# The order of the elementwise steps in the second MLP of a convolution and two-MLP kernel, and how far its output products follow

## The chip, the cores and the metric

The kernel runs on one core of a Trainium2 chip. The metric is device time in microseconds (us) of one execution: 1053.47 us before the change, the median of three runs (1053.28 to 1053.54). Within a core TensorE (PE) multiplies, ScalarE (ACT) and VectorE (DVE) do the elementwise work, and SyncE (SP) issues transfers. Each engine works through its own queue in the order in which the program was written; semaphores order the engines against one another.

## The reference

Three stages follow one another over 8192 tokens of 192 features: a causal convolution of 7 taps whose weights are a softmax, an MLP with SiLU, and an MLP with ELU (hidden width 2048 in both).

```python
def _moe_ref(x, w_in, w_out):
    h = x @ w_in
    g = h * (1.0 / (1.0 + np.exp(-h)))
    return (g @ w_out).astype(np.float32)

def _moe2_ref(x, w_in, w_out):
    h = x @ w_in
    alpha = 1.0
    g = np.where(h > 0.0, h, alpha * (np.exp(np.minimum(h, 0.0)) - 1.0))
    return (g @ w_out).astype(np.float32)

def reference(**kwargs):
    ...
    x = attn_out.reshape(B * S, D)
    x = _moe_ref(x=x, **moe_kwargs)
    return _moe2_ref(x=x, **moe2_kwargs)
```

## The kernel before

The tokens are cut into 16 blocks of 512 (`TB`, `NB`), the hidden width into 8 parts of 256 (`NQ`). A unit `u = (layer, b, q)` is one part of one block of one layer: 128 units for the SiLU layer (layer 0), then 128 for the ELU layer (layer 1). To keep precision, inputs, weights and hidden values are scaled by powers of two and held as two 16-bit floats, a high part and a low part (the remainder); products of high with high, high with low and low with high are summed.

A unit has three stages on three engines.

- PE, `in_products`: 18 matmuls that make `h`, 256 hidden rows by 512 tokens, in PSUM. They run as 9 pairs, one on each half of the array's rows. `h` has two buffers, so the products of unit u+2 need u's `h` read.
- ACT and DVE, `act_steps`. In layer 1 these are six steps: ACT copies `h` into `g` ("copy", L639), DVE takes the minimum with zero into `e` ("min", L640), ACT does the exponential of `e` in place ("exp", L643), DVE joins the two, max(e - 1, g), into `g` ("join", L644), ACT writes the scaled 16-bit high part `hi` ("high", L627, tile `g_hi`), and DVE writes the remainder `lo` ("low", L630).
- PE, the out-products: `high_products` (12 matmuls of `hi`, into the sums `c0`, `c1`, `ab0`, `ab1`, L702) and `low_ab` (4 matmuls of `lo`, L724). The rest of the low part, `low_c` (4 matmuls for each unit, L714), is kept for all eight units of a block and done at the block's end.

The order is written by hand in one loop over steps s (`tc.manual_schedule()`). In step s PE gets the in-products of unit s and then the out-products of an earlier unit, `done`: three units back (`LATE`) in most of layer 0 and in layer 1. `act_steps` spreads the six steps of a layer-1 unit over three loop steps. `running` holds what is still to be issued, so that step s puts on the queues first high and low of unit s-2, then exp and join of unit s-1, then copy and min of unit s.

At the step in which `done` is a block's last unit, PE gets `end_products`: 32 `low_c` matmuls, the last `high_products` and `low_ab`. Then the two sums are taken out of PSUM: `end_c` and `end_ab` (an ACT copy with scale and a DVE add each, `both` and `o`), and `emit_end_c` (an ACT copy across rows and a DVE add, `other`). `late = act[3:] * done[0]` puts the second half of the step's list (join, copy, min) behind the sums.

Other work of layer 1 sits at fixed steps before a block's first unit s, by `at(...)`: at s-4 `set_scale` (seven small DVE instructions, ahead of the step's own), at s-3 `split_mid` (two ACT and two DVE instructions that make the block's `x_hl`, behind the step's own, and two SP transfers, L320, that carry half of `x_hl` across the partition halves).

Buffers: in layer 1 `hi` takes half of a tile of `g_hi` or `g_lo` by turns (three tiles each), `g` one of the three `raw` tiles, `lo` one of 11 ring slots, `e` one of two. The four sums have one buffer each.

For the last unit `act_steps` issues all that is left at once, and there the high part is made by DVE (`soon`). Behind the loop stand the out-products of the last three units. In the last block the low part of `ab` is summed only then, by `last_ab` (28 matmuls in two banks).

Of the kernel before, what the change touches and what calls it, by code (L numbers as in the profile page):

```python
# [9 lines left out]
F32 = mybir.dt.float32  # L10
F32R = mybir.dt.float32r
I32 = mybir.dt.int32
I64 = mybir.dt.int64
U16 = mybir.dt.uint16
F16 = mybir.dt.float16
# [9 lines left out]
P = 128  # L25
HP = 64
TB = 512
# [3 lines left out]
NQ = DFF // (2 * P)  # L31
W_IN = 3 * P
W_OUT = 2 * D
# [12 lines left out]
def kernel(  # L46
# [17 lines left out]
    nc = tc.nc  # L64
# [3 lines left out]
    raw = ctx.enter_context(tc.tile_pool(name="raw", bufs=RAW))  # L68
# [6 lines left out]
    gp = ctx.enter_context(tc.tile_pool(name="gp", bufs=3))  # L75
# [364 lines left out]
    def scaled(layer, b):  # L440
        return layer == 1 or b >= NEW
# [82 lines left out]
    def conv_steps(b, g, acc=None):  # L524


        n = HT if g else TB

        def tap(k):
            if k == 0:  # L530
                slot = acc or (lambda: xin.tile([P, TB], F32, tag=f"conv{g}", name="conv")[:, 0:n])
                conv_t[b, g] = slot()
            x, y = x_raw[b][:, g, k : k + n], conv_t[b, g]
            w = tap_w[:, g, k : k + 1]
            if k == 0:
                nc.vector.tensor_scalar_mul(y, x, w)
            else:
                nc.vector.scalar_tensor_tensor(  # L538
                    out=y, in0=x, scalar=w, in1=y, op0=ALU.mult, op1=ALU.add
                )  # L540

        return [lambda k=k: tap(k) for k in range(TAPS)]
# [22 lines left out]
    def weights_of(u, k):  # L565
        layer, b, q = u
        return wt16[q][k] if layer == 0 and b >= NEW else wt[layer, q][k]
# [26 lines left out]
    def products(streams):  # L594
        for pair in zip(*streams):
            for f in pair:
                f()

    running = []

    def act_steps(u):

        h = h_t.pop(u)
        new = scaled(*u[:2])
        hi = gp.tile([P, 2, TB], F32R, tag=f"g_{'lo' if new and where[u] % 2 else 'hi'}", name="g_hi")
        if new:
            hi = hi.bitcast(F16)[:, :, 0:TB]
            lo = ring.tile([P, 2, TB], F16, tag=f"lo{where[u] % RING}", name="lo16")
        else:
            lo = gp.tile([P, 2, TB], F32R, tag="g_lo", name="g_lo")  # L610
        g_t[u] = hi, lo
        if new and u[0] == 1:
            g = raw.tile([P, W_IN + W_OUT], I64, tag="raw", name="g").bitcast(F32)[:, 0 : 2 * TB]
            g = g.rearrange("p (i t) -> p i t", i=2)
        else:
            g = h if u not in in_tmp else tmp.tile([P, 2, TB], F32, tag="g", name="g")
        g_of[u] = g
        if not new:
            return [
                lambda: nc.scalar.activation(out=hi, in_=h, func=ACTF.Silu),  # L620
                lambda: nc.scalar.activation(out=g, in_=h, func=ACTF.Silu),
                lambda: nc.vector.tensor_sub(out=lo, in0=g, in1=hi.bitcast(F32)),
            ]
        s = forth[u[:2]]

        def high():
            nc.scalar.activation(out=hi, in_=g, func=ACTF.Copy, scale=s)  # L627

        def low():
            nc.vector.scalar_tensor_tensor(  # L630
                out=lo, in0=g, scalar=s, in1=hi, op0=ALU.mult, op1=ALU.subtract
            )

        if u[0] == 0:
            silu = lambda: begun.append(nc.scalar.activation(out=g, in_=h, func=ACTF.Silu, scale=h_down[u[:2]]))  # L635
            return [silu, high, low]
        e = tmp.tile([P, 2, TB], F32, tag="g", name="e")
        whole = [
            lambda: begun.append(nc.scalar.activation(out=g, in_=h, func=ACTF.Copy, scale=h_down[u[:2]])),  # L639
            lambda: nc.vector.tensor_scalar_min(e, g, 0.0),  # L640
        ]
        power_of = [
            lambda: nc.scalar.activation(out=e, in_=e, func=ACTF.Exp),  # L643
            lambda: nc.vector.scalar_tensor_tensor(  # L644
                out=g, in0=e, scalar=-1.0, in1=g, op0=ALU.add, op1=ALU.max
            ),
        ]
        if u == (1, 0, 0):
            whole.insert(0, lambda: nc.scalar.activation(out=tap_s, in_=tap_s, func=ACTF.Exp, scale=0.0))
        soon = lambda: nc.vector.tensor_scalar_mul(hi, g, s)  # L650
        before = running.pop(0)[1] if len(running) > 1 else []
        if running:
            before = before + running[0][0]
        if u == units[-1]:
            hi_2, lo_2 = running[0][1]
            return before + whole + [hi_2, power_of[0], lo_2, power_of[1], soon, low]
        running.append((power_of, [high, low]))
        return before + whole

    def open_sums(u):  # L660
        for name in ("c0", "c1", "ab0", "ab1"):
            acc_t[(*u[:2], name)] = ps_a.tile([P, TB], F32, tag=name, name=name)
# [28 lines left out]
    def high_products(u, end_ab=False, end_c=False):  # L691

        layer, b, q = u
        hi, wo = g_t[u][0], weights_of(u, 1)
        if q == 0:
            open_sums(u)
        order = [("c", 1), ("ab", 0), ("ab", 2)]
        order = [(*o, i) for o in order for i in range(2)]

        def product(r, n):  # L700
            name, k, i = order[n]
            nc.tensor.matmul(  # L702
                out=acc_t[layer, b, f"{name}{r}"], lhsT=wo[ROWS[r], i, ts(k, P)], rhs=hi[ROWS[r], i, :],
                start=q == 0 and n in (0, 2), stop=end_ab and n == len(order) - 1 or end_c and n == 1,
            )

        return [[lambda r=r, n=n: product(r, n) for n in range(len(order))] for r in range(2)]

    def low_c(u, last):

        layer, b, q = u
        for i in range(2):
            for r in range(2):
                nc.tensor.matmul(  # L714
                    out=acc_t[layer, b, f"c{r}"][ROWS[i], :], lhsT=weights_of(u, 1)[ROWS[r], i, P:D],
                    rhs=g_t[u][1][ROWS[r], i, :], start=False, stop=last,
                )
# [151 lines left out]
    LAG, LATE = 2, 3  # L869
    SOLE = 7  # L870

    units = [(0, 0, 0), (0, 0, 1), (0, 1, 0), (0, 1, 1)]
# [4 lines left out]
    where = {u: s for s, u in enumerate(units)}  # L877
# [32 lines left out]
    for b in range(2, NB):  # L910
        s = where[0, b, 0]
        if b > 2:
            at(s - 14, lambda b=b: pending.extend(x_loads(b)) if b < 5 else load_x(b))
        steps = [f for fs in zip(*(conv_steps(b, g) for g in range(2))) for f in fs]
# [16 lines left out]
    for b in range(NB):  # L931
        s = where[1, b, 0]
# [26 lines left out]
    for k, q in enumerate(range(NQ)):  # L959
        s = where[0, 8 + k, 0]  # L960
# [5 lines left out]
    with tc.manual_schedule():  # L966
# [174 lines left out]
        for s in range(4, TWO + 3):  # L1141
# [4 lines left out]
            act = act_steps(units[s])  # L1146
# [20 lines left out]
        act = act_steps(units[TWO + 3])  # L1167
# [3 lines left out]
        products(out_products(units[TWO + 1]))  # L1171

        turn = where[0, NEW, 0] + LAG
        for s in range(TWO + 4, n_units):
            u = units[s]
            products(in_products(u))
            act = act_steps(u)
            done = units[s - (LATE if s > turn else LAG)]
            new, late = scaled(*done[:2]), []
            if s == turn or done[2] < NQ - 1:  # L1180
                run_fill(s)
                run(act)
                run_fill(s, 3)
                if s != turn:
                    products(high_products(done) if new else out_products(done))
                    if new and done[:2] != (1, NB - 1):
                        low_ab(done, False)
                continue
            if new:
                run_fill(s, 0)  # L1190
                late = act[3:] * done[0]
                run(act[: len(act) - len(late)])
                end_products(done)
            else:
                run(act[:1])
                products(out_products(done))
            both, end_c, end_ab = end_steps(*done[:2])
            end_c()
            if not new:
                run(act[1:])  # L1200
                run_fill(s, 0, 1)
            end_ab()
            run(late)
            if new:
                run_fill(s, 1)
            emit_end_c(*done[:2], both)
            run_fill(s, 2, 3)

        for u in units[-LATE:-1]:
            products(high_products(u))  # L1210
        for u in units[-NQ:-SOLE]:
            low_ab(u, False)
        for u in units[-NQ:-1]:
            low_c(u, False)
        products(high_products(units[-1], end_ab=True))
        low_c(units[-1], True)
        banks = [(tokens, last_ab(units[-SOLE:], tokens)) for tokens in HALF]
        both, end_c, end_ab = end_steps(1, NB - 1)
        end_ab()
# [47 lines left out]
```

## Time and profile before

| | us |
|---|---|
| median of three runs | 1053.47 |
| the profiled execution | 1051.94 |
| span of its trace, first to last instruction | 1050.1 |
| of that, layer 1 from the end of layer 0's last block on | about 520 |

The profile is one execution. Its page gives busy time by engine and the chain of work that ended last; the trace gives every instruction with its start, its length and what ended the idle time before it. The lengths of matmuls are modelled and overlap, so the pace of TensorE is read from the distance between starts of the same instruction in successive steps or blocks, not from its busy share.

### The profile page before, as it was taken

What the parts mean: (1) busy time and instruction counts of PE and PEld (TensorE: products, weight loads), DVE (VectorE), ACT (ScalarE), POOL (GpSimd) and SP (SyncE); (2) the same over time, 40 slices, a digit from 0 to 9 for tenths busy, and PEclk for the clock granted to TensorE, in tenths of its full rate; (3) what the DMA queues carried; (4) which work ended last, traced back from release to release, by engine and by line L of the source; (5) the groups of instructions that cost most, each with busy time, mean ns of one, the idle gap of its engine ahead of it and who ended that gap; (6) DMA issues with size and microseconds to landing.
All of it is one profiled execution on the core that took longest, in us unless ns stands there. A gap on an engine that the chain in (4) does not pass through costs nothing.

```text
span 1050.1 us, 23168 instructions
## 1 busy us (share of the span) xinstructions
PE 1037.2 (99%) x9763; PEld 543.2 (52%) x9763; DVE 906.9 (86%) x1321; ACT 814.7 (78%) x893; POOL 66.1 (6%) x108
## 2 busy tenths in 40 slices
PE   9999999999999999999999999999999999999996
PEld 6889844444444444444444555545544545555443
DVE  8999789888888888887679889888898888898887
ACT  7765776676777777677778888888888889888885
POOL 5420003102000000000000000000000000000000
PEclk9999999999999999999999999999999999999999
DMA  6411226334433233212122111111011110111000
GB/s 166 137 46 57 51 66 160 93 93 110 103 67 79 39 76 67 52 21 56 47 41 51 27 41 52 50 37 52 16 51 52 37 51 26 42 52 50 17 27 16
DMA packets 46519, 62.31 MB, mean 59 GB/s; under 512 B 10128, under 2 KB 29712, under 8 KB 46416
## 3 DMA queue, kind: packets, MB, share of 16 engines
q1 hardware_dynamic: 42416, 48.00, 18.5%
q0 software_dynamic: 4000, 12.85, 4.8%
q8 instruction: 76, 1.25, 0.5%
q14 instruction: 27, 0.22, 0.1%
HBM read 37.72 MB, written 12.61 MB: 48 GB/s over the span
## 4 chain that ended last, share of the span: by engine, by line
PE 72%; DVE 18%; ACT 6%; issue 3%; DMA 1%; SPq 1%; DVEq 0%
PE h L587 35%; PE ab L702 14%; PE c L702 7%; PE ab L724 7%; DVE lo L630 7%; DVE g L644 6%; ACT g_hi L627 4%; PE c L714 4%; PE ab L777 2%; PE c L777 1%; DVE e L640 1%; PE ab L683 1%; DVE x_hl L352 1%; PE c L683 1%; DVE o L825 1%
## 5 line engine op out<-in xcount | busy, mean ns | idle before, releaser
L587 PE MATMUL h<-x_hl,wi 64*128 64x512 f16 (+1 forms) x2592 | 337.4, 378 | 1.8 <-DMA x_hl<-x_hl 1.4
L587 PE MATMUL h<-x_hl,w 64*128 64x512 f16 x1872 | 220.3, 377 | 1.4 <-ACT w L250 0.7
L630 DVE SCALAR_TENSOR_TENSOR lo<-g,forth,g_hi 128x1024 f16<-128x1024 f32 x128 | 164.2, 1283 | 49.6 <-ACT g_hi L627 49.3
L627 ACT ACTIVATE g_hi<-g,forth 128x1024 f16<-128x1024 f32 x127 | 145.7, 1147 | 68.8 <-DVE g L644 68.8
L587 PEld LDWEIGHTS <-wi 64*128 64x128 f16 x2304 | 134.7, 94 | 122.5 <-issue 9.1
L635 ACT ACTIVATE h<-h,h_down 128x1024 f32<-128x1024 f32 x104 | 113.1, 1087 | 99.1 <-PE h L587 92.0
L630 DVE SCALAR_TENSOR_TENSOR lo<-h,forth,g_hi 128x1024 f16<-128x1024 f32 x104 | 133.4, 1283 | 59.7 <-ACT g_hi L627 59.7
L644 DVE SCALAR_TENSOR_TENSOR g<-e,g 128x1024 f32<-128x1024 f32 x128 | 156.0, 1219 | 1.1 <-ACT e L643 1.1
L587 PEld LDWEIGHTS <-w 64*128 64x128 f16 x1872 | 94.0, 94 | 110.1 <-issue 1.5
L702 PE MATMUL ab<-g_hi,wo 64*128 64x512 f16 x1024 | 142.9, 376 | 0.0
L639 ACT ACTIVATE g<-h,h_down 128x1024 f32<-128x1024 f32 x128 | 140.3, 1096 | 1.3 <-PE h L587 1.3
L702 PEld LDWEIGHTS <-wo 64*128 64x128 f16 x1536 | 85.0, 94 | 95.6 <-issue 21.7
L643 ACT ACTIVATE e<-e 128x1024 f32<-128x1024 f32 x128 | 133.2, 1041 | 0.8 <-DVE e L640 0.8
L627 ACT ACTIVATE g_hi<-h,forth 128x1024 f16<-128x1024 f32 x104 | 115.8, 1113 | 3.4
L702 PE MATMUL ab<-g_hi,w 64*128 64x512 f16 x832 | 107.0, 377 | 0.0
L538 DVE SCALAR_TENSOR_TENSOR conv<-x_raw,tap_w,conv 128x512 f32<-128x512 f32 (+1 forms) x174 | 102.9, 631 | 0.2
L702 PEld LDWEIGHTS <-w 64*128 64x128 f16 x1248 | 60.7, 94 | 75.2 <-issue 5.3
L640 DVE TENSOR_SCALAR e<-g 128x1024 f32<-128x1024 f32 x128 | 88.0, 688 | 2.1 <-ACT g L639 2.1
L702 PE MATMUL c<-g_hi,wo 64*128 64x512 f16 x512 | 84.9, 377 | 4.5 <-ACT g_hi L627 4.1
L724 PE MATMUL ab<-lo,wo 64*128 64x512 f16 x484 | 82.4, 377 | 0.0
L702 PE MATMUL c<-g_hi,w 64*128 64x512 f16 x416 | 62.3, 377 | 0.0
L724 PE MATMUL ab<-lo,w 64*128 64x512 f16 x416 | 62.1, 377 | 0.0
(146 smaller groups left out, 1061.4 us busy)
## 6 DMA issues: line engine op xcount, KB each, us to landing
raw<-in_w_dram POOLq DMA_DIRECT2D x16, 512.0 KB, 7.0
x_hl<-x_hl SPq DMA_DIRECT2D x62, 128.0 KB, 2.4
x_raw<-in_xT_dram SPq DMA_DIRECT2D x16, 259.0 KB, 6.1
kept_ab<-mid_ab SPq DMA_DIRECT2D x16, 256.0 KB, 2.0
raw<-in_w_dram POOLq DMA_DIRECT2D x32, 128.0 KB, 5.9
mid_ab<-kept_ab SPq DMA_DIRECT2D x16, 256.0 KB, 3.1
mid_c<-kept_c SPq DMA_DIRECT2D x32, 128.0 KB, 3.1
out_dram<-o SPq DMA_DIRECT2D x15, 256.0 KB, 2.0
```

The lines of the kernel that those rows point to most:

```text
L538: nc.vector.scalar_tensor_tensor(out=y, in0=x, scalar=w, in1=y, op0=ALU.mult, op1=ALU.add)
L587: nc.tensor.matmul(out=h[:, r, :], lhsT=w[ROWS[r], w_lo, ts(of, P)], rhs=x_part(layer, b, 3 * x_lo + part)[ROWS[r], :], start=n == 0, stop ...
L627: nc.scalar.activation(out=hi, in_=g, func=ACTF.Copy, scale=s)
L630: nc.vector.scalar_tensor_tensor(out=lo, in0=g, scalar=s, in1=hi, op0=ALU.mult, op1=ALU.subtract)
L635: silu = lambda: begun.append(nc.scalar.activation(out=g, in_=h, func=ACTF.Silu, scale=h_down[u[:2]]))
L639: lambda: begun.append(nc.scalar.activation(out=g, in_=h, func=ACTF.Copy, scale=h_down[u[:2]])),
L640: lambda: nc.vector.tensor_scalar_min(e, g, 0.0),
L643: lambda: nc.scalar.activation(out=e, in_=e, func=ACTF.Exp),
L644: lambda: nc.vector.scalar_tensor_tensor(out=g, in0=e, scalar=-1.0, in1=g, op0=ALU.add, op1=ALU.max),
L702: nc.tensor.matmul(out=acc_t[layer, b, f"{name}{r}"], lhsT=wo[ROWS[r], i, ts(k, P)], rhs=hi[ROWS[r], i, :], start=q == 0 and n in (0, 2), ...
L714: nc.tensor.matmul(out=acc_t[layer, b, f"c{r}"][ROWS[i], :], lhsT=weights_of(u, 1)[ROWS[r], i, P:D], rhs=g_t[u][1][ROWS[r], i, :], start=F ...
L724: nc.tensor.matmul(out=acc_t[layer, b, f"ab{r}"], lhsT=weights_of(u, 1)[ROWS[r], i, 0:P], rhs=g_t[u][1][ROWS[r], i, :], start=False, stop= ...
```

## The change

In layer 1 a step now issues copy and min of unit s first, then exp and join of unit s-1, then high and low of unit s-2. At a block's end the sums go on the queues ahead of that step's high and low (`late = act[-2:] * u[0]`), not ahead of join, copy and min. Out-products run four units behind instead of three from the fourth unit of layer 1 on; for that one step (`next_turn`) issues no out-products.

Two neighbouring units share one `g_hi` tile for their high parts, each in one half of it, and odd units take a `g_lo` tile for `g`, so that `hi` and `g` have six places each (`hi` had six, `g` three).

The last unit's high part is made by ACT, and the last steps are ordered by hand anew. Behind the loop stand the out-products of four units.

```diff
@@ act_steps
+        side = where[u] % 2
+        if u[0] == 0 or not side:
+            hi = gp.tile([P, 2, TB], F32R, tag=f"g_{'lo' if new and side else 'hi'}", name="g_hi")
+            hi_pair[:] = [hi.bitcast(F16)]
         if new:
-            hi = hi.bitcast(F16)[:, :, 0:TB]
+            hi = hi_pair[0][:, :, ts(side * u[0], TB)]
...
         if new and u[0] == 1:
-            g = raw.tile([P, W_IN + W_OUT], I64, tag="raw", name="g").bitcast(F32)[:, 0 : 2 * TB]
-            g = g.rearrange("p (i t) -> p i t", i=2)
+            if side:
+                g = gp.tile([P, 2, TB], F32R, tag="g_lo", name="g").bitcast(F32)
+            else:
+                g = raw.tile([P, W_IN + W_OUT], I64, tag="raw", name="g").bitcast(F32)[:, 0 : 2 * TB]
+                g = g.rearrange("p (i t) -> p i t", i=2)
...
-        soon = lambda: nc.vector.tensor_scalar_mul(hi, g, s)
-        before = running.pop(0)[1] if len(running) > 1 else []
-        if running:
-            before = before + running[0][0]
+        steps = whole + (running[-1][0] if running else [])
+        if len(running) > 1:
+            steps += running[-2][1]
+        running.append((power_of, [high, low]))
         if u == units[-1]:
-            hi_2, lo_2 = running[0][1]
-            return before + whole + [hi_2, power_of[0], lo_2, power_of[1], soon, low]
-        running.append((power_of, [high, low]))
-        return before + whole
+            (hi_1, lo_1), (hi_2, lo_2), steps = running[-2][1], steps[-2:], steps[:-2]
+            steps += [*power_of, hi_2, hi_1, lo_2, high, lo_1, low]
+        return steps
@@ the loop
+        next_turn = where[1, 0, 0] + LATE
...
-            done = units[s - (LATE if s > turn else LAG)]
+            done = units[s - LAG - (s > turn) * (LATE - LAG) - (s > next_turn)]
...
-                if s != turn:
+                if s not in (turn, next_turn):
                     products(high_products(done) if new else out_products(done))
...
-                late = act[3:] * done[0]
+                late = act[-2:] * u[0]
@@ behind the loop
-        for u in units[-LATE:-1]:
-            products(high_products(u))
+        products(high_products(units[-4]))
         for u in units[-NQ:-SOLE]:
             low_ab(u, False)
-        for u in units[-NQ:-1]:
+        for u in units[-NQ:-3]:
             low_c(u, False)
+        for u in units[-3:-1]:
+            products(high_products(u))
         products(high_products(units[-1], end_ab=True))
-        low_c(units[-1], True)
+        for u in units[-3:]:
+            low_c(u, u == units[-1])
```

## Rows read from the trace of the kernel before

**Rows 1.** The page: busy time by engine, and the chain's shares by engine.
```profile
PE 1037.2 (99%) x9763; PEld 543.2 (52%) x9763; DVE 906.9 (86%) x1321; ACT 814.7 (78%) x893; POOL 66.1 (6%) x108
PE 72%; DVE 18%; ACT 6%; issue 3%; DMA 1%; SPq 1%; DVEq 0%
```
**Rows 2.** Stretches of a block, layers 0 and 1: length, busy by engine, clock, DMA.
```profile
499.64:530.95 31.31, 31.31 (x307) 14.03 (x305) 19.14 (x29) 23.10 (x24) 0.00 (x0) 1.00 0.19 44
850.92:882.92 32.00, 31.97 (x307) 16.24 (x306) 28.54 (x37) 27.66 (x30) 0.00 (x0) 1.00 0.15 42
```
**Rows 3.** The chain in order of time, one unit of layer 1: start, us, what.
```profile
848.15 1.15 DVE g L644
...
849.33 1.16 ACT g_hi L627
...
850.51 1.28 DVE lo L630
851.79 1.15 DVE g L644
```
**Rows 4.** Timeline of TensorE, starts of blocks' `low_c`: start, us, [idle before].
```profile
530.95 1.92 PE L714 MATMUL c<-lo,w 64*64 64x512 f16 x32
...
562.39 1.92 PE L714 MATMUL c<-lo,wo 64*64 64x512 f16 x32
...
1010.88 1.92 PE L714 MATMUL c<-lo,wo 64*64 64x512 f16 x32
```
**Rows 5.** Timeline of TensorE, in-products: a block's end step, and an ordinary step.
```profile
528.91 2.11 PE L587 MATMUL h<-x_hl,wi 64*128 64x512 f16 x18
...
534.54 2.11 PE L587 MATMUL h<-x_hl,wi 64*128 64x512 f16 x18
...
538.21 2.11 PE L587 MATMUL h<-x_hl,wi 64*128 64x512 f16 x18
...
541.88 2.10 PE L587 MATMUL h<-x_hl,wi 64*128 64x512 f16 x18
```
**Rows 6.** Timeline of ScalarE, one step of layer 1 and a sum.
```profile
850.38 1.04 ACT L643 ACTIVATE e<-e 128x1024 f32<-128x1024 f32 x1
851.33 1.09 ACT L639 ACTIVATE g<-h,h_down 128x1024 f32<-128x1024 f32 x1
...
854.97 0.67 ACT L834 ACTIVATE both<-c,back 128x512 f32<-128x512 f32 x1
```
**Rows 7.** Timeline of VectorE: `min`, first of `set_scale`, the step behind it, a split.
```profile
861.76 0.69 DVE L640 TENSOR_SCALAR e<-g 128x1024 f32<-128x1024 f32 x1
862.36 0.41 DVE L484 TENSOR_REDUCE total<-all 128x1 f32<-128x256 f32 x1
...
863.71 1.28 DVE L630 SCALAR_TENSOR_TENSOR lo<-g,forth,g_hi 128x1024 f16<-128x1024 f32 x1
...
870.28 0.75 DVE L352 SCALAR_TENSOR_TENSOR x_hl<-mid_ab,x_up,x_hl 128x512 f16<-128x512 f32 x1
```
**Rows 8.** Crossing of `x_hl`: ACT's second write, SP's issue, TensorE, landing times.
```profile
773.22 0.71 ACT L351 ACTIVATE x_hl<-mid_c,x_up 128x512 f16<-128x512 f32 x1
...
774.54 1.30 SPq L320 DMA_DIRECT2D x_hl<-x_hl  x2
...
776.96 1.24 PE L587 MATMUL h<-x_hl,wi 64*128 64x512 f16 x9
779.33 1.24 PE L587 MATMUL h<-x_hl,wi 64*128 64x512 f16 x9 [1.13 <-DMA x_hl<-x_hl]
...
DMA to landing us min/median/max: 2.0/2.4/5.1
```
**Rows 9.** Timeline of TensorE, the end of the kernel.
```profile
1037.60 0.61 PE L702 MATMUL c<-g_hi,wo 64*128 64x512 f16 x4 [2.16 <-ACT g_hi L627]
...
1039.43 1.71 PE L714 MATMUL c<-lo,wo 64*64 64x512 f16 x28
...
1042.81 3.23 PE L741 MATMUL last<-lo,wo 128*128 128x256 f16 x28
```

More of the change, by code (lines that the diff above doesn't have):

```diff
@@ L599 @@
     running = []
+    hi_pair = []
     def act_steps(u):
@@ L604, in act_steps @@
         new = scaled(*u[:2])
-        hi = gp.tile([P, 2, TB], F32R, tag=f"g_{'lo' if new and where[u] % 2 else 'hi'}", name="g_hi")
+        side = where[u] % 2
+        if u[0] == 0 or not side:
+            hi = gp.tile([P, 2, TB], F32R, tag=f"g_{'lo' if new and side else 'hi'}", name="g_hi")
+            hi_pair[:] = [hi.bitcast(F16)]
         if new:
-            hi = hi.bitcast(F16)[:, :, 0:TB]
+            hi = hi_pair[0][:, :, ts(side * u[0], TB)]
             lo = ring.tile([P, 2, TB], F16, tag=f"lo{where[u] % RING}", name="lo16")
```

## The prediction, made before the change was run

> **What bounds the kernel now.** I read the page first. It shows TensorE at 99% and a chain of which 72% is TensorE [rows 1], which would leave an elementwise reordering nothing to win. But matmul lengths are modelled and overlap, so I looked at the pace next. The same eight units take 31.31 us in layer 0 and 32.00 us in layer 1, both "full" by TensorE's busy time, at a granted clock of 1.00, the full 2.4 GHz, both times [rows 2]. Both blocks have the same matmuls in number and size. So 0.69 us of each layer-1 block is not TensorE's own work. TensorE's own pace in layer 1 is seen just behind the layer boundary, before the other engines have fallen back: an ordinary step takes 541.88 - 538.21 = 3.67 us and a block's end step 534.54 - 528.91 = 5.63 us [rows 5]; 7 x 3.67 + 5.63 = 31.32 us, which is layer 0's block.
>
> What takes the 32.00 us is in the chain: late in layer 1 it holds no TensorE at all, only join (DVE), high (ACT), low (DVE), join again, 3.64 us a turn [rows 3]. That is a ring closed by the order of the queues. Low of unit s-2 waits for high of the same unit, join of s-1 stands behind that low on DVE, and the next high waits for that join. ACT and DVE are busy for only 27.66 and 28.54 us of the block [rows 2], but neither can use its free time, because each waits for the other. The ring's 3.64 us is just under TensorE's 3.67 us, so it loses nothing in an ordinary step. What stands on the ring besides (the sums, `set_scale`, the split) it cannot win back, and so the ring, not TensorE, sets 32.00 us a block.
>
> **The ordinary step.** Nothing is added or removed: three ACT and three DVE instructions per unit, as before. In the new order a step's first instruction, copy, waits for TensorE; min waits for this copy; exp needs the min of the step before, high the join of the step before, and low the high just ahead. Nothing that ACT waits for in a step is made by DVE in the same step, so the ring is open. ACT then needs 1.09 + 1.04 + 1.16 = 3.29 us [rows 3, 6], DVE 0.69 + 1.15 + 1.28 = 3.12 us [rows 3, 7], both under TensorE's 3.67. The price is that copy, behind which exp and high are queued, now waits for TensorE at the head of ACT's queue. That costs nothing as long as the out-products come late enough: high of unit u is written in step u+2 and read in step u+4, more than one step of 3.67 us later. With three units behind, that reserve would be a fraction of a step; the fourth unit is its cover.
>
> **The end step.** From the start of its in-products: they end at 1.94, copy at 3.0, exp at 4.1. TensorE finishes `c` at 1.94 + 1.86 (the `low_c`) + 0.43 = 4.2 and `ab` at 5.5. ACT's two sums take 0.67 each [rows 6], DVE's I take at 0.75, as the split of the same size [rows 7]: `c` is free at 5.7, `ab` at 7.0. The next block writes them at 5.5 + 1.94 = 7.5 and at 7.9. So 0.9 us are left for `ab`, the tightest place on PSUM. High, behind the sums now, ends at 7.4, low at 8.7; they are needed at 11.1 and 12.4.
>
> **Scale and split.** `set_scale` takes 863.71 - 862.36 = 1.35 us of DVE [rows 7] a step after the sums, the split 1.5 us a step later. With them DVE needs 4.5 and 4.6 us in two steps of 3.67, and runs up to 2 us behind; it wins 0.55 us a step back over the rest of the block. By the same walk low is then still some 2.6 us ahead of TensorE's need for it. DVE's backlog also moves the crossing of `x_hl`. Adding the lengths up (other ends at 9.4, `set_scale` at 10.8, two steps' work at 17.0, the split at 17.8), SP issues it 2.4 us ahead of the next block's first in-products, at 20.2. With the instructions overlapping at their ends, as they do in the timeline, it is 3.1. Before, it is 776.96 - 774.54 = 2.42 us [rows 8]. TensorE needs it 0.97 us into these in-products. The second transfer goes out 0.65 us behind the first and lands 2.4 us later in the median, 5.1 at worst [rows 8]. So the median has room, and a stray one like the 1.13 us wait in rows 8 stays possible. I count nothing for it, and 0 to 2 us in the range.
>
> **The buffers.** Six places for `g` instead of three, and as many for `hi`: the reader of a place is done steps before the next writer. That two units share a tile, in interleaved halves, could order a write of one half behind a read of the other. Before, ACT writes the third part of `x_hl` at 773.22 while the transfer that reads parts one and four of the same tile goes out only at 774.54, and does not wait for it [rows 8]: interleaved parts are kept apart. I take 0; the other end is in the rivals.
>
> **The sum.** (1) Blocks. From the `low_c` of layer 1's first block to that of its 15th are 1010.88 - 562.39 = 448.49 us [rows 4]. At 31.31 us, 14 blocks take 438.34: **-10.15**. (2) The fourth unit. The first `low_c` comes one unit later in the stream, and the step ahead of it has in-products only: 534.54 + 1.94 + 7 x 3.67 + 2.04 = 564.21 against 562.39 [rows 4, 5]: **+1.82**. (3) The end. From the last `low_c` in the loop to the last matmul are now 1042.81 + 3.23 - 1010.88 = 35.16 us [rows 4, 9], with waits such as the 2.16 us for high, because the ring paces the last steps too, whose TensorE work is short. A pair of matmuls is 3.67 / 17 = 0.216 us. New: the rest of the end step 3.59; four steps of 15 pairs (the last block leaves out `low_ab`), 12.96; then high 1.30, `low_ab` 0.43, five units' `low_c` 1.22 (20/28 of 1.71), three times high 3.89, three units' `low_c` 0.73, `last_ab` 3.23 [rows 9]. Together 27.35: **-7.81**. I walked the elementwise steps beside this. The last copy ends 1.1 us after the last in-products; the three highs that are left end 4.1, 5.1 and 6.2 us after them and are needed at 4.2, 5.6 and 6.8; the last low ends at about 8.0 and is needed at 8.1. DVE's high, 0.75 us shorter to wait for in principle, is not missed. This fits so closely that 0.5 us may be lost. What follows the last matmul, 1050.1 - 1046.04 = 4.06 us, stays.
>
> Sum: -16.1 us. The profiled execution goes from 1051.94 to 1035.8 us. The median of the runs is 1.53 us above the profiled one; I keep that and forecast **1037.3 us**, 1.5% less.
>
> **A rule weighed.** 17 pairs in 3.67 us are 216 ns for each pair of 512 columns, at the granted clock of 1.00, step after step [rows 2, 5], also in layer 0, where ACT is busy for only 23 of 31 us. The Trainium skill (TensorE: Matmul & The Clock Gate, Back-to-back issue gap) gives a formula that comes to the same 216 ns, but calls it the gap of isolated matmuls and says that a sustained stream reaches about 131 ns; by that TensorE would have no floor at 3.67 us and the sum would end at DVE's busy time. The trace speaks against it: no step shorter than the formula's is seen in either layer. It stands as the last rival.
>
> **Rivals and chances.**
> (a) Forecast, TensorE bound at 31.2 to 31.5 us a block, 1034.5 to 1041 us: 0.84. TensorE's pace beside elementwise engines that no longer pause is not in the trace; the nearest rows bound it by 31.31 (layer 0) and, if half of what layer 1 loses stays, 31.65 [rows 2].
> (b) Part of the loss stays at one place per block, the `ab` bank with its 0.9 us or the crossing: 0.4 us x 14 = 5.6, giving 1043. Against it: both walks leave room. 0.06.
> (c) The shared tile orders halves after all. Then the first products behind the loop, due 1.3 us after the last in-products, wait for the neighbour's high, ready at 4.1: 2.8 us, giving 1040. 0.03.
> (d) Another ring takes the place of the old and nothing changes, 1053.5: it would need DVE to make within a step what ACT waits for in it, and no pair of steps does. 0.03.
> (e) Slower: the crossing. If DVE's backlog leaves 3.75 us from issue to need, and both transfers land as late as the worst row, 0.65 + 5.1 = 5.75, TensorE stands 2.0 us in each of 15 blocks: +30, 1067 us. It outweighs the gain from 1.1 us a block on, a landing of 4.2 us every time. The median is 2.4, and one of 15 blocks shows a wait. 0.03.
> (f) TensorE is faster once fed: DVE's 28.5 us a block would bind, 14 x 2.8 = 39 us less again, 998 us. 0.01.
>
> Faster by over 0.2% (about what a measurement of this kernel tells from no change) hold (a), (b), (c) and (f): 0.94. Within: 0.03. Slower: 0.03. For 8 in 10 the range takes in (a)'s bounds and reaches over (b) and (c): 1034 to 1043.5 us.
>
> **What the profile after would show.** Blocks of layer 1 at 31.3 us between `low_c` starts; a chain of TensorE down to the last products, without DVE-ACT rings; ACT idle ahead of copy, released by TensorE; DVE idle by some 2.8 us a block, mostly ahead of min and low; no waits of 2 us for high at the end, and about 27.4 us from the last `low_c` of the loop to the last matmul. Blocks still at 32.0 with idle TensorE ahead of the first in-products would mean (b) or (e); waits on `g_hi` ahead of even units' out-products (c).

## The result and the profile after

The changed kernel takes 1038.2 us in the median (four runs, 1037.97 to 1038.64) against 1053.49 us before: a ratio of 0.9856, 95% interval 0.9839 to 0.9873, 1.4% less. The forecast was 1037.3 us. The profiled execution took 1037.99 us; its span is 1036.3 us, 13.8 us under the span before.

The page of the changed kernel, busy time by engine and the chain's shares, beside [rows 1]:

```profile
PE 1028.6 (99%) x9763; PEld 524.5 (51%) x9763; DVE 908.1 (88%) x1320; ACT 818.5 (79%) x894; POOL 66.1 (6%) x108
PE 95%; DVE 2%; ACT 1%; issue 1%; DMA 0%; SPq 0%; POOL 0%; DVEq 0%; POOLq 0%
```

TensorE's busy share is 99% in both kernels and says nothing. The chain says it: TensorE's part went from 72% to 95%, DVE's from 18% to 2%. The same in one block of layer 1 (stretch: length, busy time of PE, PEld, DVE, ACT, POOL, granted clock, DMA), beside [rows 2]:

```profile
816.84:848.15 31.31, 31.31 (x306) 14.03 (x304) 28.72 (x37) 27.88 (x29) 0.00 (x0) 1.00 0.15 43
```

The elementwise engines do the same 28.7 and 27.9 us of work, in 31.31 us instead of 32.00. That is layer 0's block. What ACT waits for in the 14 blocks from the first `low_c` of layer 1 to the last, first in the kernel before, then in the changed one (the list of waits: us in total, times, longest):

```profile
ACT g_hi L627 <- DVE g L644: 60.1, 98, 1.2
```

```profile
ACT g L646 <- PE h L587: 33.3, 57, 0.9
ACT o L840 <- PE ab L730: 8.5, 14, 0.6
ACT both L840 <- PE c L708: 4.5, 14, 0.3
```

Before, high waited for DVE's join, 98 times; now ACT waits for TensorE alone. The ring is gone and the order of waiting is the one wanted: elementwise work behind TensorE. The chain in order of time shows it in the changed kernel's ordinary step, beside [rows 3]:

```profile
827.93 1.94 PE h L587 x18
829.88 0.43 PE c L708 x4
830.31 0.86 PE ab L708 x8
831.17 0.43 PE ab L730 x4
831.60 1.94 PE h L587 x18
```

831.60 - 827.93 = 3.67 us, TensorE with no pause. Starts of `low_c` in the timeline of TensorE, beside [rows 4]; the first is that of layer 0's last block, the last that of layer 1's 15th:

```profile
530.88 1.92 PE L720 MATMUL c<-lo,w 64*64 64x512 f16 x32
...
565.98 1.92 PE L720 MATMUL c<-lo,wo 64*64 64x512 f16 x32
...
597.29 1.92 PE L720 MATMUL c<-lo,wo 64*64 64x512 f16 x32
...
628.98 1.92 PE L720 MATMUL c<-lo,wo 64*64 64x512 f16 x32
...
848.15 1.92 PE L720 MATMUL c<-lo,wo 64*64 64x512 f16 x32
...
879.74 1.92 PE L720 MATMUL c<-lo,wo 64*64 64x512 f16 x32
...
1004.98 1.92 PE L720 MATMUL c<-lo,wo 64*64 64x512 f16 x32
...
1029.31 3.23 PE L747 MATMUL last<-lo,wo 128*128 128x256 f16 x28
```

Twelve of the 14 blocks take 31.31 us; the two that end at 628.98 and 879.74 take 31.69 and 31.59. From these rows the 13.8 us divide as follows.

| | before | after | difference | forecast |
|---|---|---|---|---|
| first `low_c` of layer 1 at | 562.39 | 565.98 | +3.59 | +1.82 |
| from there to the 15th `low_c` | 448.49 | 439.00 | -9.49 | -10.15 |
| from there to the end of the last matmul | 35.16 | 27.56 | -7.60 | -7.81 |
| from there to the end of the span | 4.06 | 3.76 | -0.30 | 0 |
| sum | | | -13.80 | -16.14 |

The 2.3 us that are missing lie in the first two lines. All but about 0.1 us of them are waits for the crossing of `x_hl`; the worst is at layer 1's second block. The transfer's issue on SP, and TensorE's in-products of that block, beside [rows 8]:

```profile
550.69 1.30 SPq L320 DMA_DIRECT2D x_hl<-x_hl  x2
...
551.17 1.04 PE L587 MATMUL h<-x_hl,wi 64*128 64x512 f16 x8
553.18 0.37 PE L587 MATMUL h<-x_hl,wi 64*128 64x512 f16 x1 [0.97 <-DMA x_hl<-x_hl]
553.81 1.24 PE L587 MATMUL h<-x_hl,wi 64*128 64x512 f16 x9 [0.25 <-DMA x_hl<-x_hl]
```

Here the crossing goes out only 0.48 us ahead of the in-products. The next in-products start at 556.41, 5.24 us behind these instead of 3.67. In the next block the lead is 584.25 - 581.33 = 2.92 us:

```profile
581.33 1.30 SPq L320 DMA_DIRECT2D x_hl<-x_hl  x2
...
584.25 2.10 PE L587 MATMUL h<-x_hl,wi 64*128 64x512 f16 x18
```

One reason stands in DVE's timeline ahead of it: between low and the next min, DVE finds the maximum of layer 0's last block (two reductions, 541.50 to 542.69) and then does `set_scale`, 2.5 us in one piece, and everything behind it comes later, the split too.

```profile
541.50 0.68 DVE L423 TENSOR_REDUCE sum<-mid_ab 128x1 f32<-128x512 f32 x1
542.09 0.67 DVE L423 TENSOR_REDUCE sum<-other 64x1 f32<-64x512 f32 x1
542.69 0.40 DVE L484 TENSOR_REDUCE total<-all 128x1 f32<-128x256 f32 x1
...
544.01 0.69 DVE L647 TENSOR_SCALAR e<-g 128x1024 f32<-128x1024 f32 x1
```

In the two blocks that take 31.69 and 31.59 us the lead is 2.92 us too, but there the two transfers land 3.6 and 3.5 us after their issue (the median of the pair), where 2.4 is usual.

### The profile page after: what moved, and what is told of

Same layout as the page of the kernel before. It is cut to its first block, busy times and chain, and to the rows that moved or that the text cites. A ratio compares the mean times of both kernels' runs of the same rounds, so it can differ in the third digit from the quotient of the medians.

```text
span 1036.3 us, 23166 instructions
## 1 busy us (share of the span) xinstructions
PE 1028.6 (99%) x9763; PEld 524.5 (51%) x9763; DVE 908.1 (88%) x1320; ACT 818.5 (79%) x894; POOL 66.1 (6%) x108
## 4 chain that ended last, share of the span: by engine, by line
PE 95%; DVE 2%; ACT 1%; issue 1%; DMA 0%; SPq 0%; POOL 0%; DVEq 0%; POOLq 0%
PE h L587 46%; PE ab L708 19%; PE c L708 10%; PE ab L730 9%; PE c L720 5%; PE ab L783 2%; PE c L783 1%; PE ab L689 1%; PE c L689 1%; DMA x_hl<-x_hl 0%; PE warm L977 0%; DVE lo L637 0%; PE conv_ps L1008 0%; DVE g L651 0%; ACT g_hi L634 0%
## 5 line engine op out<-in xcount | busy, mean ns | idle before, releaser
L587 PE MATMUL h<-x_hl,wi 64*128 64x512 f16 (+1 forms) x2592 | 330.0, 378 | 1.4 <-DMA x_hl<-x_hl 1.4
L587 PEld LDWEIGHTS <-wi 64*128 64x128 f16 x2304 | 114.8, 94 | 136.9 <-issue 2.5
L708 PE MATMUL ab<-g_hi,wo 64*128 64x512 f16 x1024 | 133.2, 376 | 0.0
L708 PEld LDWEIGHTS <-wo 64*128 64x128 f16 x1536 | 75.2, 94 | 92.7 <-issue 6.6
L708 PE MATMUL c<-g_hi,wo 64*128 64x512 f16 x512 | 78.1, 377 | 0.0
L730 PE MATMUL ab<-lo,wo 64*128 64x512 f16 x484 | 73.8, 376 | 0.0
```

What stands on the lines that cost most here:

```text
L587: nc.tensor.matmul(out=h[:, r, :], lhsT=w[ROWS[r], w_lo, ts(of, P)], rhs=x_part(layer, b, 3 * x_lo + part)[ROWS[r], :], start=n == 0, stop ...
L708: nc.tensor.matmul(out=acc_t[layer, b, f"{name}{r}"], lhsT=wo[ROWS[r], i, ts(k, P)], rhs=hi[ROWS[r], i, :], start=q == 0 and n in (0, 2), ...
L730: nc.tensor.matmul(out=acc_t[layer, b, f"ab{r}"], lhsT=weights_of(u, 1)[ROWS[r], i, 0:P], rhs=g_t[u][1][ROWS[r], i, :], start=False, stop= ...
```

## Experiments

My theory was that the old order closes a ring of DVE and ACT, that the new order opens it, that four units' distance and six places for `g` are what the new order needs, and that TensorE then sets the pace. The rivals were that the distance alone does it, that the order alone does it, and that the places and the sums are by-work. Each experiment undoes one part of the changed kernel, unless it says otherwise. The kernel before ran beside each group: 1053.62 us (15 runs, 1051.57 to 1054.02) beside the old order, the new order three behind, the three places and the sums; 1052.72 us (7 runs) beside the changed kernel again, the last units in turn, the split and the whole of min more before the change; 1051.9 us (7 runs) beside the other three with more of min.

### The changed kernel again

> The changed kernel once more, beside the next ones on the same chip: 1038.2 us again within 0.5 us, with TensorE waiting for the crossing of layer 1's second block by about 1 us and blocks of 31.31 us otherwise.

Measured: 1038.94 us (four runs, 1037.78 to 1039.36), ratio 0.9871 (0.9854 to 0.9887), 0.2 us more than was expected at most. The profile shows the same two waits for the crossing at layer 1's second block, 0.97 and 0.25 us; of the 14 blocks one is late (31.55 us) instead of two. The runs spread by 1.6 us, which is nearly as much as the effect of the split at the head of its step; that experiment is read from its runs' spread and its trace together.

### The old order, four units behind

```diff
-        steps = whole + (running[-1][0] if running else [])
-        if len(running) > 1:
-            steps += running[-2][1]
+        older = running[-2][1] if len(running) > 1 else []
+        newer = running[-1][0] if running else []
+        steps = older + newer + whole if u != units[-1] else whole + newer + older
...
-                late = act[-2:] * u[0]
+                late = act[3:] * done[0]
```

> The changed kernel with the old order in layer 1's loop (high and low of unit s-2 first, copy and min of unit s last, sums where they were); six places for g, four units behind and the new last unit stay. Theory 1 (the ring join, high, low closed by the order sets the block): blocks of layer 1 go back to 31.9 to 32.5 us, the last steps are paced by the ring again, 1050 to 1057 us in all, with the chain on DVE and ACT. Theory 2 (the gain comes from out-products standing four units behind, which gives TensorE more slack): blocks stay at 31.3, 1037 to 1040 us.

Measured: 1057.7 us (1057.54 to 1058.05), ratio 1.0042 (1.0027 to 1.0057): slower than before the change, with all that the change gives but the order. One block, and the chain inside another:

```profile
859.49:892.19 32.70, 32.00 (x306) 18.82 (x304) 28.64 (x37) 27.78 (x30) 0.00 (x0) 1.00 0.14 42
```

```profile
846.96 1.16 ACT g_hi L634
...
848.14 1.28 DVE lo L637
849.43 1.15 DVE g L651
...
851.78 1.28 DVE lo L637
```

The ring is back with its 3.64 us a turn (851.78 - 848.14, from low to low) and the block is 32.70 us, 0.2 over what was expected; the time is 0.7 us over its range. Theory 1 holds: the distance alone brings nothing. That it is worse than before the change fits the sums lying one step later, right ahead of `set_scale`, so that the ring carries both in a row; this was read from the chain and not tried by itself.

### The new order, three units behind

```diff
-            done = units[s - LAG - (s > turn) * (LATE - LAG) - (s > next_turn)]
+            done = units[s - LAG - (s > turn) * (LATE - LAG)]
...
-                if s not in (turn, next_turn):
+                if s != turn:
...
-        products(high_products(units[-4]))
```

> The changed kernel with out-products three units behind in layer 1. Theory 1 (the new order needs the fourth unit as cover: high of unit u is written in step u+2 some 3.2 us after the in-products and would be read 3.7 us after them, which DVE's backlog of up to 2 us behind sums, set_scale and split exceeds): blocks of 32.2 to 32.8 us, waits of TensorE for high or low a few times a block, 1050 to 1058 us. Theory 2 (the order alone opens the ring and is enough): 31.3 us a block, 1037 to 1041 us.

Measured: 1052.2 us (1052.12 to 1052.4), ratio 0.9993 (0.9983 to 1.0003): no gain at all. Blocks take 32.18 us (822.34, 854.51, 886.70). TensorE's waits, and one of them in its timeline:

```profile
PE ab L730 <- DVE lo L637: 7.5, 15, 1.6
```

```profile
869.54 0.61 PE L730 MATMUL ab<-lo,wo 64*128 64x512 f16 x4 [0.43 <-DVE lo L637]
```

Fifteen waits in 15 blocks, each for a low. In the block shown the listed wait is 0.43 us of the 0.87 that the block is over 31.31; the rest is in small pauses of the same step and the two before it, which take 3.72, 3.88 and 4.27 us. The chain leads from that low back along DVE, `set_scale` in it, to the sums of the block just ended: DVE's backlog, as the prediction had it. Theory 1 holds: order and distance only work together.

### Three places for g

```diff
-            if side:
-                g = gp.tile([P, 2, TB], F32R, tag="g_lo", name="g").bitcast(F32)
-            else:
-                g = raw.tile([P, W_IN + W_OUT], I64, tag="raw", name="g").bitcast(F32)[:, 0 : 2 * TB]
-                g = g.rearrange("p (i t) -> p i t", i=2)
+            g = raw.tile([P, W_IN + W_OUT], I64, tag="raw", name="g").bitcast(F32)[:, 0 : 2 * TB]
+            g = g.rearrange("p (i t) -> p i t", i=2)
```

> The changed kernel with g in the three raw tiles only, as before the change. Theory 1 (the new order then closes another ring: copy of unit u+3, first in ACT's step, must wait for low of unit u, last in DVE's step before, so copy, exp, high, low stand in line, about 4.4 us a step): 36 to 38 us a block, 1110 to 1140 us, ACT's copy waiting for DVE's low. Theory 2 (the places are only a convenience, three are enough because a unit lives for three steps): 1038 to 1042 us.

Measured: 1153.37 us (1153.31 to 1153.44), ratio 1.0948 (1.0926 to 1.097). Theory 1 by kind, and more than its range. ACT's largest wait and TensorE's, and the turn of the new ring (timelines of ACT and of DVE):

```profile
ACT g L643 <- DVE lo L634: 164.3, 123, 2.4
PE c L705 <- ACT both L837: 44.3, 15, 3.0
```

```profile
865.08 1.11 ACT L643 ACTIVATE g<-h,h_down 128x1024 f32<-128x1024 f32 x1 [1.51 <-DVE lo L634]
866.10 1.05 ACT L647 ACTIVATE e<-e 128x1024 f32<-128x1024 f32 x1
...
869.69 1.11 ACT L643 ACTIVATE g<-h,h_down 128x1024 f32<-128x1024 f32 x1 [1.51 <-DVE lo L634]
```

```profile
867.17 1.23 DVE L648 SCALAR_TENSOR_TENSOR g<-e,g 128x1024 f32<-128x1024 f32 x1 [0.25 <-ACT e L647]
868.32 1.28 DVE L634 SCALAR_TENSOR_TENSOR lo<-g,forth,g_hi 128x1024 f16<-128x1024 f32 x1
```

Copy waits for the place that low frees, exp follows copy, join waits for exp, low stands behind join, and the next copy waits for it: 869.69 - 865.08 = 4.61 us a turn, 38.4 us a block. I had expected 4.4 by way of high; the ring goes by way of join. ACT, late by that, also takes the sums late, and TensorE waits 3.0 us for them in 15 blocks. So the new order can't do without the six places. Places for `hi` were not taken away by themselves.

### The sums behind high and low

```diff
-                late = act[-2:] * u[0]
+                late = []
```

> The changed kernel with a block's sums behind the step's high and low instead of ahead of them. Theory 1 (ab's bank has 0.9 us to spare, and high and low ahead of the sums take it just about up): 0 to 0.3 us a block, 1038 to 1042 us. Theory 2 (the place of the sums is what frees the block's end): TensorE waits for the banks by about the 1.1 to 1.3 us of a high or low in each block, 1053 to 1057 us.

Measured: 1038.21 us (1037.75 to 1038.62), ratio 0.9856 (0.984 to 0.9873): the same as the changed kernel. DVE's end of the `ab` sum, and TensorE's first write into that bank:

```profile
853.16 0.74 DVE L831 SCALAR_TENSOR_TENSOR o<-ab,back,o 128x512 f32<-128x512 f32 x1
```

```profile
853.92 1.05 PE L708 MATMUL ab<-g_hi,wo 64*128 64x512 f16 x8
```

853.90 against 853.92: nothing to spare, and next to nothing lost (blocks of 31.33 us instead of 31.31). This part of the change is margin, not gain.

### The last units in turn

```diff
-            steps += [*power_of, hi_2, hi_1, lo_2, high, lo_1, low]
+            steps += [hi_2, lo_2, *power_of, hi_1, lo_1, high, low]
```

> The changed kernel with the remaining highs and lows in unit order at the very end (high, low of unit n-3, then exp and join of the last, then high, low of n-2, high, low of n-1). Theory 1 (the end fits closely: join of the last unit then stands behind a low of 1.2 us, and its high is 0.6 us late for TensorE): 1038.5 to 1039.5 us. Theory 2 (the order by hand at the end carries most of the 7.6 us gained there): 1042 us or more.

Measured: 1038.35 us (1038.22 to 1038.96), ratio 0.9865 (0.985 to 0.988), not to be told from the changed kernel. From the last `low_c` of the loop (1005.02) to the end of the last matmul it is 27.74 us against 27.56: 0.2 us, less than the 0.6 expected.

```profile
1029.53 3.23 PE L747 MATMUL last<-lo,wo 128*128 128x256 f16 x28
```

So the end's 7.6 us don't come from the order in which the last highs and lows are issued. The old order with four units behind has 29.89 us there (1022.42 to 1049.08 + 3.23), the new order with three 31.47 (1015.44 to 1043.68 + 3.23), the kernel before 35.16: the order in the loop and the distance both have a part in it. All three runs have the new order of TensorE's products behind the loop and the last high on ACT; what these bring was not tried by itself.

### The split at the head of its step

```diff
-        at(s - 3, lambda b=b: split_mid(b), 3)
+        at(s - 3, lambda b=b: split_mid(b), 0 if b else 3)
```

> The changed kernel with the split of x_hl at the head of its step instead of behind it, for all blocks of layer 1 but the first. Theory 1 (what is left over TensorE's pace, some 2.5 us between the sum of the prediction and the trace, are waits for the crossing, most of it at the second block where DVE has the last layer-0 block's maximum to find as well): the crossing goes out about 3 us earlier, no wait for it is left, 1035.3 to 1036.5 us. Theory 2 (those waits are made up later, or the split ahead of copy delays TensorE instead): 1038 us or more.

Measured: 1036.4 us (four runs, 1036.36 to 1036.53), ratio to before 0.9846 (0.9831 to 0.986). The changed kernel beside it has 1037.78 to 1039.36; the runs don't overlap, and this is the fastest kernel of the study. Its crossing at the second block, what is left of waiting there, and the first and last `low_c` of the 14 blocks:

```profile
547.91 1.75 SPq L320 DMA_DIRECT2D x_hl<-x_hl  x2
```

```profile
551.49 0.61 PE L730 MATMUL ab<-lo,wo 64*128 64x512 f16 x4 [0.41 <-DVE lo L637]
...
564.98 1.92 PE L720 MATMUL c<-lo,wo 64*64 64x512 f16 x32
...
1003.32 1.92 PE L720 MATMUL c<-lo,wo 64*64 64x512 f16 x32
```

The crossing goes out 2.8 us earlier, no wait for one is left in layer 1, and 14 blocks take 1003.32 - 564.98 = 438.34 us, the figure of the forecast. Theory 1 holds: with the span at 1034.6 us, 1.7 of the 2.3 us between sum and trace are back. The rest is mostly the step with the wait for low shown here, 4.26 us instead of 3.67. It comes with the edit: the split now stands ahead of that low on DVE, which ends at 551.44, where it ended at 549.96 in the changed kernel and TensorE did not wait for it.

### More work for DVE, before and after the change

Four runs repeat min, the whole of it or half, in the kernel before and in the changed one.

```diff
-            lambda: nc.vector.tensor_scalar_min(e, g, 0.0),
+            lambda: (nc.vector.tensor_scalar_min(e, g, 0.0), nc.vector.tensor_scalar_min(e, g, 0.0)),
```

In the half versions the second instruction has `e[:, 0, :]` and `g[:, 0, :]`.

The whole, before:

> The kernel before the change with min done twice in each layer-1 unit, 0.6 us more of DVE a unit, 4.8 us a block. Theory 1 (a ring sets the block, and DVE stands idle 0.61 us between min and low in each turn of it): the second min falls into that gap and costs under 0.5 us a block, 1053 to 1061 us in all, DVE busy for 33 of 32 to 32.5 us only by overlapping ends. Theory 2 (DVE's work sets the block): 4 us or more a block, 1110 us or more.

The half, before:

> The kernel before the change with half of min done a second time in each layer-1 unit, 0.34 us more of DVE a unit, less than the 0.61 us for which DVE waits for high in each turn of the ring. Theory 1 (in the five ordinary steps it falls into that gap; in the three steps with sums, set_scale and split the gap is taken already and it lies on the ring): 0.6 to 1.2 us a block, 1063 to 1072 us. Theory 2 (DVE's work counts in full): 2.7 us a block, 1094 us or more. Theory 3 (all of it is hidden): 1053 to 1056 us.

The half, after:

> The changed kernel with half of min done a second time in each layer-1 unit: 0.34 us more of DVE a unit, 2.7 us a block, just what DVE has free there (31.3 less 28.5). Theory 1 (TensorE sets the block and DVE's free time can be used, because nothing in a step waits in a ring): 0 to 0.4 us a block, 1038 to 1044 us, blocks of 31.3 us but where the crossing comes late. Theory 2 (another ring stands just under TensorE's pace): 1.5 us or more a block, 1060 us or more.

The whole, after:

> The changed kernel with the whole of min done twice, 0.6 to 0.65 us more of DVE a unit, about 5 us a block, more than DVE has free. Theory 1 (TensorE bound up to DVE's busy time, then DVE bound): DVE's 28.5 + 5 = 33.5 to 34 us set the block, 1070 to 1080 us, and the chain is DVE's without a pause. The same edit on the kernel before took 34.5 us a block and 1096 us. Theory 2 (a ring through DVE and ACT remains and the edit lengthens it): 35 us a block, 1095 us or more.

| | before the change | changed |
|---|---|---|
| half of min more | 1073.36 us, 21.5 more; block 33.35 | 1047.42 us, 9.2 more; blocks mostly 31.73, the first 32.9 |
| whole of min more | 1096.0 us, 43.3 more; blocks mostly 34.84 | 1081.04 us, 42.8 more; blocks mostly 33.86 |

All four are misses, three of them by little: the half lies 1.4 us over its range before and 3.4 after, the whole in the changed kernel 1 us. One reason is the size of the dose, the work added. DVE's timeline with the half in the changed kernel:

```profile
862.90 1.15 DVE L647 TENSOR_SCALAR e<-g 128x1024 f32<-128x1024 f32 x2
863.97 1.22 DVE L651 SCALAR_TENSOR_TENSOR g<-e,g 128x1024 f32<-128x1024 f32 x1
```

Both instructions together hold DVE for 1.07 us where one holds it for 0.60: the half costs 0.47 us a unit, 3.7 us a block, not the 2.7 that I worked out, and more than the 2.6 us that DVE has free. Two whole mins hold it for 1.33 us (859.10 to 860.43 in the changed kernel), so the whole costs 0.73 us a unit and not 0.6 to 0.65. The whole before missed by 35 us: it could not fall into the ring's gap of 0.61 us, and 28.5 + 8 x 0.73 = 34.4 us of DVE do not fit into a block of 32.0 anyway. What the runs do show is what becomes of DVE's free time. A block of each with the half, the old kernel first:

```profile
830.91:864.26 33.35, 32.44 (x306) 15.74 (x304) 31.85 (x45) 28.28 (x30) 0.00 (x0) 1.00 0.14 41
```

```profile
822.33:854.06 31.73, 31.68 (x306) 14.90 (x306) 31.31 (x45) 28.10 (x29) 0.00 (x0) 1.00 0.15 43
```

The old block gets 1.35 us longer and DVE still stands idle for 1.5 us of it: over 14 blocks it waits 8.8 us for high and 4.6 for ACT's sums. The changed block gets 0.42 us longer and DVE waits for nothing but 0.2 us in 14 blocks. So the half is already enough to make DVE the bound of the changed kernel, while the old one can't use all of DVE's time. TensorE pays at the crossing, which goes out 1.82 us ahead in the block shown (838.78 to 840.60) instead of 2.92. With the whole, both pay 43 us, for both are then bound by DVE, the old one nearly (the gap ahead of low is gone: e, e, lo, g follow one another, and DVE waits only at the sums, 0.57 us a block). How large a dose the changed kernel takes for nothing was not found.

## Why the prediction was right, step by step

**The bound.** Right. That the paces of blocks differ, 31.31 against 32.00, and that the chain has no TensorE in it, was the reading that decided; the busy share pointed the other way. The ring was shown by bringing it back: 1057.7 us with the old order alone.

**The ordinary step.** Right in both halves. Nothing that ACT waits for in the 14 blocks is made by DVE, and TensorE runs at 3.67 us. The fourth unit as its cover was argued in the prediction and is shown by the new order three units behind, which gains nothing (1052.2 us).

**The end step.** The margin for `ab` was put at 0.9 us. In the changed kernel's last block end the DVE add ends at 1010.24 and the bank is written at 1010.95: 0.7 us. Without the sums' new place it is 0.02, and still next to no wait.

**Scale, split and crossing.** The lead of the crossing was put between 2.4 and 3.1 us; it is 2.92 where the walk applies. The step that failed is "I count nothing for it, and 0 to 2 us in the range": at layer 1's second block the lead is 0.48 us, because the walk took the ordinary block for all and left out what is special to the first: the search for layer 0's last maximum, 1.2 us of DVE just there, and the step without out-products, by which TensorE comes 3.67 - 1.94 = 1.7 us sooner: 2.9 us in sum, against a lead that is 2.44 us shorter. How the two share the loss was not tried. That cost 1.8 us (565.98 against 564.14, the forecast less the 0.07 us by which layer 0 ended earlier), and two stray landings 0.4 and 0.3. Rival (b) in its crossing form thus happened, at three blocks instead of 14.

**The buffers.** The prediction asked whether the new places bring waits and found none, rightly; rival (c) can be dropped, for TensorE waits for no high. It did not ask what the old places would have cost. That is the largest figure of the study, 115 us.

**The end.** 27.56 us against 27.35 worked out. The walk that left 0.1 us of margin held; DVE's high for the last unit is not missed.

**The sum.** -16.1 us against -13.8 in the spans, -15.3 in the medians. The median came within 0.9 us of the forecast partly by luck: the sum was 2.3 us too large, and the 1.53 us that the prediction kept between profiled execution and median did not stay (0.2 in the changed kernel). In the kernel before such a difference goes with TensorE's clock. Of its 15 runs beside the first experiments, nine with a mean granted clock of 0.998 took 1053.21 to 1054.02 us, six with 1.000 took 1051.57 to 1052.05; the profiled execution has 1.000, and so have all four runs of the changed kernel. At the same granted clock the change is thus worth 13.8 us, 1.3%. The rest of the 15.3 fits a fall of the clock that the changed kernel's runs don't have; for the other runs of the kernel before in that comparison the clock is not on record.

**The rule weighed.** TensorE kept 3.67 us for 17 pairs where nothing held it back, block after block, so the 131 ns a matmul that the Trainium skill (TensorE: Matmul & The Clock Gate, Back-to-back issue gap) gives for a sustained stream was not seen here; 216 ns is the pace of a sustained stream of 512-column pairs in this kernel. Rival (f) can be dropped.

## What to carry to other kernels

Read a pipelined engine's bound from the distance between equal instructions in equal blocks: two stretches with the same matmuls and different lengths show a loss that a busy share of 99% hides. Where two engines are each under 90% busy and wait for each other by turns, look for a ring in the order of their queues, and count for each new order how many buffers and how much distance it needs; here order, distance and places gave 15 us together, and each of the three, taken away alone, cost nearly all of that or far more. Walk the first block by itself: it is where work of the stage before still lies in the queue.

## What the runs showed of the hardware

With three places for `g`, TensorE stands still behind a block's end, 3.0 us ahead of the first matmul into the `c` sums and 0.97 ahead of the next, and then runs at half clock for some 3 us. Stretches of 1 us around one such place (the eighth column is the granted clock: 1.00 is 2.4 GHz, 0.50 is 1.2 GHz):

```profile
883.00:884.00 1.00, 0.21 (x2) 0.00 (x0) 0.42 (x1) 0.48 (x1) 0.00 (x0) 1.00 0.00 0
...
887.00:888.00 1.00, 0.45 (x4) 0.20 (x4) 1.00 (x2) 0.98 (x2) 0.00 (x0) 0.50 0.00 0
888.00:889.00 1.00, 1.00 (x8) 0.52 (x6) 1.00 (x2) 0.42 (x1) 0.00 (x0) 0.50 0.00 0
```

```profile
887.96 2.31 PE L705 MATMUL ab<-g_hi,wo 64*128 64x512 f16 x8
```

The wait is paid a second time: in the timeline the 8 `ab` matmuls behind it take 2.31 us, where they take 1.03 at full clock. In the blocks of the other kernels that are shown here the granted clock is 1.00. The clock falls behind shorter waits too. The kernel before with min twice waits 1.77 and 2.27 us for high in its last steps, and behind the second wait stands:

```profile
1082.00:1084.00 2.00, 2.00 (x14) 0.60 (x14) 1.89 (x3) 0.12 (x1) 0.00 (x0) 0.50 0.00 0
```

The kernel before has waits of 1.91 and 2.16 us at the same place, with no fall of the clock in the execution that was traced. That its runs with a mean of 0.998 lose the clock there is likely and not shown, for no trace of one is kept. The changed kernel has no such waits.

An instruction on half the elements is not half an instruction: a record of min on 1024 elements is 0.69 us long, on 512 elements 0.43. Two that write the same tile in a row overlap less: the second min starts 0.72 us behind the first (862.90 to 863.62), where join, which writes another tile, starts 0.60 us behind a single min (544.01 to 544.61) and 0.35 behind the half (863.62 to 863.97).
